# Tile addresses, load order and the head's instruction order in an SSD-scan and SiLU-MLP kernel on one core

## The chip, the cores and the metric

The kernel runs on one core of one Trainium2 chip. A core has a matrix engine (PE, whose weight loads are shown apart as PEld), a vector engine (DVE), an activation engine (ACT), a general engine (POOL) and a queue engine (SP) that issues transfers (DMA). The engines run side by side; each works through its own instructions in the order in which the program lists them, and waits where an operand isn't there yet. The metric is the device time in microseconds of one execution, the lower the better. It is given as the median of runs.

## The reference, cut to what matters

Two parts follow each other. The first is a state-space scan: for each of 4 batches and 8 heads, 768 positions with decay `a`, inputs `x` (32 wide), `B` and `C` (16 wide).

```python
log_a = np.log(np.clip(a, 1e-06, 1.0))
for c in range(nc):                       # chunks of the sequence
    la = log_a[:, :, sl]
    cum = np.cumsum(la, axis=-1)
    L = np.exp(cum[:, :, :, None] - cum[:, :, None, :]) * causal
    M = np.einsum('bhin,bhjn->bhij', Cc, Bc) * L
    y_intra = np.einsum('bhij,bhjd->bhid', M, xc)
    y_inter = np.einsum('bhin,bhnd->bhid', Cc, state) * decay_to_i
    y[:, :, sl] = y_intra + y_inter
    state = decay_full * state + np.sum(Bx, axis=2)
```

Its output, seen as 3072 rows of 256, goes through a two-layer network in float32:

```python
h = x @ w_in                              # (3072, 256) @ (256, 2048)
g = h * (1.0 / (1.0 + np.exp(-h)))
return g @ w_out                          # (3072, 2048) @ (2048, 256)
```

The weights arrive as float64, so that the kernel reads them as pairs of 32-bit words.

## The kernel before

**The scan.** The 3072 positions are cut into 12 units of 256 positions, three for each batch, and a unit into four chunks of 64. For each unit the kernel loads prefix inputs (`load_pa`, tile pz), decays with zeroed chunk starts (`load_ab`, tile ab), B and C (`load_n`, one layout, tiles bn and tbc; `load_t`, another layout, for the first unit of the first batch and from unit 3 on), and x (`load_x`, tile xt). The decays of units 2 and later come from two arrays in device memory, a_in and a_zero, which the kernel itself writes once, in `f_A2` (lines 246 to 253), after clipping `a` on DVE.

The letters in the schedule name a unit's steps. T is the transpose of B and C (`f_T` on DVE, L352, or `f_TP` on PE), with the two masked copies ce on ACT (L370). P is the prefix scan on DVE (L311), C multiplies C by it (L374, tile cw). The digits 1 and 2 are the two halves of the decay scan E on DVE (L324), B the product BT (L347). D is two groups of small matmuls on PE (`f_G` L402, `f_D0` L390). S updates the states on DVE (L420, L422), s masks them on ACT (L429), M multiplies into E on DVE (L408). Y is the output's matmuls on PE (L442, L451) and its copy to tile xf on ACT (L461). The letters h, l and d split xf into three parts, xh on ACT (L474) and xl, xd on DVE (L477, L481). These three parts of x, for two units together, are 4 KB per partition each and live in the pool `quad`, six buffers which they share with the raw weights.

**The weights.** They come in 16 slices of 256 columns or rows, eight for each layer: `load_w(n)` loads slice n into a `quad` buffer (512 KB), `w_size` prepares two words on ACT (L176, L179), `w_bits` combines them on DVE (L184, L186, L187) and adds on POOL (L192) to give a float32 slice. `w_bits(n)` also issues the load of slice n + 6, whose buffer it frees. `w_h`, `w_l` and `w_d` make three parts of the slice (wh on ACT, L199; wl and wd on DVE, L203 and L208), each a block of 2 KB per partition.

**The network.** The first two units, half an iteration, multiply float32 slices: `f_s1` (L491) for the first layer, `f_s2` (L504) for the second. A float32 matmul is two passes on PE, and each pass shows as one record. The ten units after them run as five iterations P of 16 steps each. A step works on 128 columns of the inner width and 512 positions, with float32r matmuls, which are one pass each: `s1_d` multiplies xd by wd (L518, 2 matmuls), ACT rescales (L520), `s1_h` adds xh by wh and xl by wl (L526, 4), ACT applies SiLU and splits (L534, L536), DVE or POOL make gl (L540) and DVE gd (L544). Three steps later `s2` multiplies gh by wh and gl by wl (L558, L559, 2 each), and `s2_d` multiplies gd by wd (L572, 2). In all of them the activations are the streamed operand and the weights the loaded one. `PLAN` and `FIRST` say which scan letters of the next two units are woven into which step, and `ASIDE` in which steps POOL makes gl.

The order is written out by hand. Below the line `w_size(5)` (680), the list `steps` gives pairs of a unit and a slice for `f_s1` and, as text, what follows each; a second list does the same around the `f_s2` calls (m0 to m5). In these texts "2:C12B" means the letters C, 1, 2 and B of unit 2, "L" a unit's loads, b, s, h, l and d with a number `w_bits`, `w_size`, `w_h`, `w_l` and `w_d`. All loads are issued by SP, in the order of the program, and a load whose buffer or source isn't ready holds up those behind it.

**Addresses.** The pools are laid out in the order in which they are created, so that a pool's place sets the addresses of those behind it. The parts of x and the raw weights (`quad`) begin at byte 32,576 of the partition, which is 832 past a multiple of 1024; the 76 blocks of 2 KB (pool `blk`, everything that `block()` makes: g's parts, the weights' parts, xf) begin at byte 72,576, 896 past a multiple of 1024. All sizes are multiples of 1024 from there, so every tile of a kind has the same offset.

Of the kernel before, what the change touches and what calls it, by code (L numbers as in the profile page):

```python
# [8 lines left out]
FP32 = mybir.dt.float32  # L9
# [24 lines left out]
def kernel(  # L34
# [26 lines left out]
    Q = 64  # L61
# [9 lines left out]
    loads = ctx.enter_context(tc.tile_pool(name="loads", bufs=1))  # L71
    quad = ctx.enter_context(tc.tile_pool(name="quad", bufs=6))
    sc = ctx.enter_context(tc.tile_pool(name="sc", bufs=1))
    sc2 = ctx.enter_context(tc.tile_pool(name="sc2", bufs=2))
    blk = ctx.enter_context(tc.tile_pool(name="blk", bufs=1))
    dram = ctx.enter_context(tc.tile_pool(name="dram", bufs=1, space=bass.MemoryType.DRAM))
    ps_s = ctx.enter_context(tc.tile_pool(name="ps_s", bufs=1, space=bass.MemoryType.PSUM))
# [3 lines left out]
    ctx.enter_context(tc.manual_schedule())  # L81

    NB = 76

# [18 lines left out]
    def load_pa(u, q):  # L103
        for c in range(4):
            q.dma_start(out=pz[:, c, 1:], in_=a_in[4 * u + c].rearrange("h (o t) -> h o t", o=1).to_broadcast([H, N, Q]))

# [16 lines left out]
    def load_t(u, i, q):  # L123
        b, t0 = at(u)
        if u == 0:
            tbc[u] = block("tbc0").rearrange("p (i e r n) -> p i e r n", i=2, e=2, r=8)
        elif u not in tbc:
            tbc[u] = loads.tile([128, 2, 2, 8, N], FP32, name="tbc")
        for g in range(4):
            q.dma_start(out=tbc[u][32 * g:32 * g + 32, i],  # L130
                        in_=(B, C)[i][b, 2 * g:2 * g + 2, t0:t0 + UT].rearrange("e (t r) n -> t e r n", r=8))

    def load_x(u, q):
        b, t0 = at(u)
        xt[u] = loads.tile([128, 2, H, D], FP32, name="xt", bufs=2)
        for k in range(2):
            q.dma_start(out=xt[u][:, k], in_=x[b, :, t0 + 128 * k:t0 + 128 * k + 128].rearrange("h p d -> p h d"))

    def load_unit(u):
        load_pa(u, nc.sync)  # L140
        if 0 < u < UPB:
            load_n(u, 1, nc.sync)
        else:
            load_t(u, 0, nc.sync)
            load_t(u, 1, nc.sync)
        load_n(u, 0, nc.sync)
        load_ab(u, nc.sync)
        load_x(u, nc.sync)
# [32 lines left out]
    def w_bits(n, parts=1):  # L181
        if n in raw:
# [7 lines left out]
            for i in range(parts):  # L190
                fs = slice(WF // parts * i, WF // parts * (i + 1))
                nc.gpsimd.tensor_tensor(out=two(w32[n])[:, :, fs].bitcast(U32), in0=u[:, :, fs], in1=v[:, :, fs],  # L192
                                        op=ALU.add)
        if n + RAW < NW:
            load_w(n + RAW, nc.sync)
# [15 lines left out]

    a_in = dram.tile([batch * S // Q, H, Q], FP32, name="a_in")
    a_zero = dram.tile([batch * S // Q, H, Q], FP32, name="a_zero")
# [32 lines left out]
    def f_A2():  # L246

        r = slice(0, NC0 * batch)
        nc.vector.tensor_scalar(out=acl[r], in0=acl[r], scalar1=1.0, scalar2=1e-6, op0=ALU.min, op1=ALU.max)
# [31 lines left out]
    tiny = const.tile([128, 1], FP32, name="tiny")  # L281
    nc.scalar.activation(tiny, idle[:, 0:1], AF.Silu)
    busy(5)
# [32 lines left out]
    def f_P(u):  # L316
        if u < 2:
            f_P0(u)
        f_P1(u)
# [15 lines left out]
    def f_Ek(u, k):  # L335
        scan_E(u, H * k, H, ab.pop((u, k)))
# [311 lines left out]
    f_Y(0)  # L648
    f_P(1)
    f_Ek(1, 0)  # L650
# [8 lines left out]
    f_s1(0, 1)  # L659
    f_Ek(1, 1)  # L660
    f_B(1)
    w_bits(2, 2)
# [19 lines left out]
    def stage(u, what):  # L682
        for c in what:
            if c == "L":
                load_unit(u)
            elif c == "T":
                if 0 < u < UPB:
# [31 lines left out]
            elif c == "d":  # L719
                f_xd(u)  # L720

    def todo(text):

        for step in text.split():
            if ":" in step:
                u, what = step.split(":")
                stage(int(u), what)
                continue
            n = int(step[1:].split(".")[0])
            {"b": w_bits, "s": w_size, "h": w_h, "l": w_l, "d": w_d, "m": f_s2, "o": f_out0}[step[0]](n)  # L730
# [24 lines left out]
    def step(s):  # L755
# [6 lines left out]
        if t >= 0:  # L762
            PENDING.append(t)
        if s == 0:
            s1_d(0)

        if s < last:
# [86 lines left out]
```

## Time and profile before

| | |
|---|---|
| median of 3 runs | 349.0 us (347.99 to 350.06) |
| the profiled execution's own time | 348.75 us |
| its span, first to last instruction | 346.5 us |
| granted PE clock, mean | 0.995 |
| PE busy | 324.6 us, 94% |
| DVE busy | 262.6 us, 76% |
| ACT busy | 211.9 us, 61% |
| POOL busy | 66.1 us, 19% |
| DMA, mean rate | 77 GB/s, 26.66 MB moved |

A busy time is the sum of an engine's instructions in the profiled execution. In a table of waits each row names the waiting engine, tile and line, then who released it, the total in microseconds, how often, and the longest. A piece of the chain has its start, its length and what ran; the pieces lie end to end, so that a piece of several matmuls divided by their number is the time from one start to the next. A matmul's own duration in the profile is longer than that, about 0.39 us, since matmuls overlap. L12 is line 12 of the kernel before.

### The profile page before, as it was taken

To read this page: it belongs to the slowest core of one execution; us is meant where nothing else is said; L and a number is where in the kernel's file an instruction comes from. 1 tells how busy PE (TensorE), PEld (TensorE's weight loads), DVE (VectorE), ACT (ScalarE), POOL (GpSimd) and SP (SyncE) were. 2 spreads that over 40 slices of the span, in tenths; PEclk is the share of its full clock that TensorE was granted. 3 is DMA by queue.
4 is the path that set the end of the run, shared out by engine and by line. 5 is a ranking of instruction groups with operands and counts; after the bars stand their busy time and mean duration, and the time that the engine had idled before them with its cause. 6 is when DMAs were issued, how large, how long until landed. Compare 5 with 4: busy or idle time off the path is not lost.

```text
span 346.5 us, 7826 instructions
## 1 busy us (share of the span) xinstructions
PE 324.6 (94%) x3145; PEld 254.3 (73%) x3146; DVE 262.6 (76%) x430; ACT 211.9 (61%) x403; POOL 66.1 (19%) x56
## 2 busy tenths in 40 slices
PE   8977999777998999999999999999999999999991
PEld 4566788666866778777778778778778788788881
DVE  7969975999559998898766896965996853674443
ACT  3656575432467877757775756666676756555651
POOL 3235523120113010242101231202250202000000
PEclk9999999999999999999999999999999999999998
DMA  6975894650171160045340163420153000020003
GB/s 121 209 248 173 168 335 98 145 115 0 48 144 25 38 117 1 18 108 83 67 97 0 34 120 67 88 63 1 48 112 57 2 2 0 0 48 14 0 0 63
DMA packets 99339, 26.66 MB, mean 77 GB/s; under 512 B 87558, under 2 KB 92422, under 8 KB 99302
## 3 DMA queue, kind: packets, MB, share of 16 engines
q1 hardware_dynamic: 95110, 25.76, 33.1%
q10 hardware_dynamic: 4192, 0.39, 0.9%
q8 instruction: 24, 0.39, 0.5%
q14 instruction: 13, 0.11, 0.1%
HBM read 22.80 MB, written 3.34 MB: 75 GB/s over the span
## 4 chain that ended last, share of the span: by engine, by line
PE 70%; DVE 10%; DMA 8%; SPq 8%; issue 2%; ACT 1%; DVEq 0%; ACTq 0%
PE hp L526 22%; PE b L572 11%; PE hp L518 10%; PE oa L559 10%; PE oa L558 10%; DMA raw<-in_moe_w_out_dram 3%; SPq L121 3%; PE oa L504 2%; DVE wl L203 2%; PE gy L451 2%; DMA ab<-a_zero 2%; PE gy L442 1%; DMA a_in<-acl 1%; DMA raw<-in_moe_w_in_dram 1%; PE gy L402 1%
## 5 line engine op out<-in xcount | busy, mean ns | idle before, releaser
L520 ACT ACTIVATE hp<-hp 128x512 f32<-128x512 f32 x80 | 46.6, 582 | 75.0 <-PE hp L518 74.7
L540 DVE TENSOR_TENSOR gl<-g,gh 128x512 fp32r<-128x512 f32 x56 | 38.6, 689 | 47.7 <-ACT gh L536 44.8
L540 POOL TENSOR_TENSOR gl<-g,gh 128x512 fp32r<-128x512 f32 x24 | 39.9, 1663 | 172.4 <-ACT gh L536 156.3
L526 PE MATMUL hp<-xh,wh 128*128 128x512 f32 x160 | 65.6, 410 | 2.6 <-ACT hp L520 2.6
L544 DVE SCALAR_TENSOR_TENSOR gd<-gh,g 128x512 fp32r<-128x512 f32 x80 | 61.9, 776 | 6.0 <-ACT gh L536 6.0
L526 PE MATMUL hp<-xl,wl 128*128 128x512 f32 x160 | 63.2, 395 | 0.0
L559 PE MATMUL oa<-gl,wl 128*128 128x512 f32 x160 | 63.1, 394 | 0.0
L558 PE MATMUL oa<-gh,wh 128*128 128x512 f32 x160 | 62.7, 392 | 0.0
L536 ACT ACTIVATE gh<-g 128x512 fp32r<-128x512 f32 x80 | 50.6, 632 | 2.8
L518 PE MATMUL hp<-xd,wd 128*128 128x512 f32 x160 | 50.4, 396 | 0.0
L534 ACT ACTIVATE g<-hp 128x512 f32<-128x512 f32 x80 | 47.5, 594 | 0.6 <-PE hp L526 0.6
L572 PE MATMUL b<-gd,wd 128*128 128x512 f32 x160 | 44.6, 391 | 0.0
L526 PEld LDWEIGHTS hp<-xh,wh 128*128 128x128 f32 x160 | 30.0, 188 | 13.0 <-ACT hp L520 6.0
L558 PEld LDWEIGHTS oa<-gh,wh 128*128 128x128 f32 x160 | 30.0, 188 | 7.5 <-ACT o L584 0.7
L518 PEld LDWEIGHTS hp<-xd,wd 128*128 128x128 f32 x160 | 30.0, 188 | 7.3
L559 PEld LDWEIGHTS oa<-gl,wl 128*128 128x128 f32 x160 | 30.0, 188 | 7.2
L572 PEld LDWEIGHTS b<-gd,wd 128*128 128x128 f32 x160 | 30.0, 188 | 6.8 <-DVE o L599 0.2
L526 PEld LDWEIGHTS hp<-xl,wl 128*128 128x128 f32 x160 | 30.1, 188 | 5.5
L491 PE MATMUL hp<-xf,w 128*128 128x256 f32 x128 | 30.1, 386 | 4.3 <-POOL w L192 3.0
L192 POOL TENSOR_TENSOR w<-wu,wv 128x512 uint32<-128x512 uint32 (+1 forms) x20 | 23.4, 1178 | 50.5 <-DVE wv L187 47.8
L491 PEld LDWEIGHTS hp<-xf,w 128*128 128x128 f32 x128 | 23.5, 190 | 9.7 <-POOL w L192 4.5
L324 DVE TENSOR_TENSOR_SCAN E<-ab,diag 128x512 f32<-128x512 f32 x24 | 28.7, 1228 | 0.7 <-DMA ab<-a_zero 0.7
(80 smaller groups left out, 367.0 us busy)
## 6 DMA issues: line engine op xcount, KB each, us to landing
ab<-a_zero SPq DMA_DIRECT2D x40, 128.0 KB
raw<-in_moe_w_in_dram SPq DMA_DIRECT2D x8, 512.0 KB
raw<-in_moe_w_out_dram SPq DMA_DIRECT2D x8, 512.0 KB
xt<-in_x_dram SPq DMA_DIRECT2D x24, 128.0 KB
out_dram<-ot SPq DMA_DIRECT2D x44, 64.0 KB
bn<-in_B_dram SPq DMA_DIRECT2D x22, 64.0 KB
tbc<-in_C_dram SPq DMA_DIRECT2D x40, 32.0 KB
pz<-a_in SPq DMA_DIRECT2D x40, 32.0 KB
```

Of the source, the lines that this page charges most:

```text
L324: nc.vector.tensor_tensor_scan(out=E[u].rearrange("p k h t -> p (k h t)")[:, Q * g0:Q * (g0 + n)], data0=t.rearrange("p g t -> p (g t)"), ...
L491: nc.tensor.matmul(out=hp[:, i], lhsT=two(w32[j])[:, kc, 128 * i:128 * i + 128], rhs=two(XF[u])[:, kc], start=(kc == 0), stop=(kc == KC - 1))
L518: nc.tensor.matmul(out=HP[s], lhsT=two(WD[f // 2])[:, kc, 128 * (f % 2):128 * (f % 2) + 128], rhs=XD[P][:, kc], start=(kc == 0), stop=Fals ...
L520: nc.scalar.activation(HP[s], HP[s], AF.Copy, scale=-HALF / UP)
L526: nc.tensor.matmul(out=HP[s], lhsT=two(w[f // 2])[:, kc, 128 * (f % 2):128 * (f % 2) + 128], rhs=x_[P][:, kc], start=False, stop=(kc == KC ...
L534: nc.scalar.activation(G[s], HP.pop(s), AF.Silu, scale=UP)
L536: nc.scalar.activation(GH[s], G[s], AF.Copy, scale=DOWN)
L540: engine.tensor_tensor(out=GL[s], in0=G[s], in1=GH[s].bitcast(FP32), op=ALU.subtract)
L544: nc.vector.scalar_tensor_tensor(out=GD[s], in0=GH[s].bitcast(FP32), scalar=1.0 + 1.0 / HALF, in1=G.pop(s), op0=ALU.mult, op1=ALU.subtract)
L558: nc.tensor.matmul(out=OA[P][m], lhsT=two(WH[n])[:, r, ms], rhs=gh, start=(f == 0), stop=False)
L559: nc.tensor.matmul(out=OA[P][m], lhsT=two(WL[n])[:, r, ms], rhs=gl, start=False, stop=(f == NF - 1))
L572: nc.tensor.matmul(out=B2[P][:, m], lhsT=two(WD[n])[:, r, 128 * m:128 * m + 128], rhs=gd, start=(fresh and s == tiles[0]), stop=True, skip ...
```

## The change

Four things are edited.

- The pool `quad` is created behind `blk`, and a tile of 160 bytes that nothing uses is added in pool `sc`; a tile of one element (`tiny`) is gone. The blocks then begin at byte 48,128 and the parts of x at byte 203,776, both multiples of 1024.
- `load_pa` becomes one transfer in place of four. For that a_in is laid out by head, with 65 values for each chunk, the first of them zero; `f_A2` writes the other 64, and a new transfer writes the zeros from a zeroed tile. `load_t` becomes two transfers in place of four.
- The loads of unit 2 and 3 are split and spread: C, B and x of unit 2 are issued ahead of slice 3's `w_bits` and of `f_A2`, its decays behind slice 4's; then C (with B in the layout of `load_t`) and x of unit 3; the decays and bn of unit 3 follow unit 2's scan ("3:A"). `w_bits` issues the next load only up to slice 4; slices 11 to 15 have their own letter r in the lists.
- In the head, unit 1's prefix scan stands behind its second decay scan, slice 3's `w_bits` before `f_A2`, unit 3's steps P, C, 1, 2 and B one place earlier and before slice 12's bits, its D before the second `f_s2`; the splits of unit 2 and 3 follow in another order; and the first `s1_d` (letter p) comes after m3 instead of after m5.

```diff
+    quad = ctx.enter_context(tc.tile_pool(name="quad", bufs=6))
+    sc.tile([128, 40], FP32, name="pad")
...
-        for c in range(4):
-            q.dma_start(out=pz[:, c, 1:], in_=a_in[4 * u + c].rearrange("h (o t) -> h o t", o=1).to_broadcast([H, N, Q]))
+        q.dma_start(out=pz.rearrange("p c t -> p (c t)"),
+                    in_=a_in[:, 4 * u:4 * u + 4].rearrange("h (o c) t -> h o (c t)", o=1).to_broadcast([H, N, 4 * Q + 4]))
...
-        for g in range(4):
-            q.dma_start(out=tbc[u][32 * g:32 * g + 32, i],
-                        in_=(B, C)[i][b, 2 * g:2 * g + 2, t0:t0 + UT].rearrange("e (t r) n -> t e r n", r=8))
+        src = (B, C)[i]
+        for e in range(2):
+            q.dma_start(out=tbc[u][:, i, e].rearrange("p r n -> p (r n)"),
+                        in_=bass.AP(tensor=src.tensor, offset=src.offset + ((b * H + e) * S + t0) * N,
+                                    ap=[[2 * S * N, 4], [8 * N, 32], [1, 8 * N]]))
...
+    def load_bcx(u, what="bcx"):
+        if "c" in what:
+            if 0 < u < UPB:
+                load_n(u, 1, nc.sync)
+            else:
+                load_t(u, 0, nc.sync)
+                load_t(u, 1, nc.sync)
+        if "b" in what:
+            load_n(u, 0, nc.sync)
+        if "x" in what:
+            load_x(u, nc.sync)
...
-        if n + RAW < NW:
+        if n < 5:
             load_w(n + RAW, nc.sync)
...
-    a_in = dram.tile([batch * S // Q, H, Q], FP32, name="a_in")
+    a_in = dram.tile([H, batch * S // Q, Q + 1], FP32, name="a_in")
...
-        nc.sync.dma_start(out=a_in, in_=acl[r])
+        nc.sync.dma_start(out=a_in[:, :, 1:].rearrange("h c t -> c h t"), in_=acl[r])
...
+    nc.sync.dma_start(out=a_in[:, :, 0:1].rearrange("h c t -> c h t"),
+                      in_=misc[:NC0 * batch, 0:H].rearrange("p (h t) -> p h t", t=1))
...
-    f_P(1)
     f_Ek(1, 0)
...
     f_Ek(1, 1)
+    f_P(1)
...
+    load_bcx(2)
+    w_bits(3, 2)
     f_A2()
-    load_unit(2)
     w_size(4, "u")
-    w_bits(3, 2)
...
     w_bits(4)
+    load_pa(2, nc.sync)
+    load_ab(2, nc.sync)
+    load_bcx(3, "cx")
     w_size(5)
...
+            elif c == "A":
+                load_pa(u, nc.sync)
+                load_bcx(u, "b")
+                load_ab(u, nc.sync)
...
-    steps = ((1, 0, ""), (0, 3, "b5 s6"), (1, 1, "b6 s7"), (1, 2, "b7 s8"), (1, 3, "b8"), (0, 4, "2:T"),
-             (1, 4, "2:P"), (0, 5, "2:C12B s9 3:L"), (1, 5, "2:D b9 s10"), (0, 6, "2:SsM"), (1, 6, "b10 s11"),
-             (0, 7, "2:Y b11 s12 3:T"), (1, 7, "b12 s13 3:P h0"))
+    steps = ((1, 0, ""), (0, 3, "b5 r11 s6"), (1, 1, "b6 s7"), (1, 2, "b7 s8"), (1, 3, "b8"), (0, 4, "2:T"),
+             (1, 4, "2:P"), (0, 5, "2:C12B s9 3:A r12 r13"), (1, 5, "2:D b9 r14 r15 s10"), (0, 6, "2:SsM"), (1, 6, "b10 s11"),
+             (0, 7, "2:Y b11 s12 3:T"), (1, 7, "3:PC12B b12 s13 h0"))
...
-    for text in ("m0 3:C12B 2:h h1 l0 d0 2:l b13 s14", "m1 3:D 2:d 4:L h2 l1 d1 b14 s15", "m2 3:SsM h3 l2 d2 b15",
-                 "m3 3:Y h4 l3 d3", "m4 3:h h5 l4 d4 h8 3:l", "m5 3:d l5 d5 4:T l8 d8"):
+    for text in ("m0 3:D 4:L 3:SsM 2:h h1 2:l 2:d l0 d0 b13 s14", "m1 h2 l1 d1 b14 s15", "m2 3:Y 3:h l2 d2 3:l 3:d b15 h3",
+                 "m3 l3 d3 h4 p0", "m4 h8 l4 d4 h5 l8 d8", "m5 4:T l5 d5"):
...
-        if s == 0:
-            s1_d(0)
```

More of the change, by code (lines that the diff above doesn't have):

```diff
@@ L71 @@
     loads = ctx.enter_context(tc.tile_pool(name="loads", bufs=1))
-    quad = ctx.enter_context(tc.tile_pool(name="quad", bufs=6))
     sc = ctx.enter_context(tc.tile_pool(name="sc", bufs=1))
@@ L137, in load_x @@
             q.dma_start(out=xt[u][:, k], in_=x[b, :, t0 + 128 * k:t0 + 128 * k + 128].rearrange("h p d -> p h d"))
+    def load_bcx(u, what="bcx"):
[9 more added lines that the diff above has]
+            load_x(u, nc.sync)
     def load_unit(u):
         load_pa(u, nc.sync)
[L141 to L146, printed above, removed]
+        load_bcx(u, "bc")
         load_ab(u, nc.sync)
@@ L280 @@
                                 fill=1.0, base=-64 * c, channel_multiplier=1)
-    tiny = const.tile([128, 1], FP32, name="tiny")
-    nc.scalar.activation(tiny, idle[:, 0:1], AF.Silu)
+    nc.scalar.activation(misc[:, 2 * UT - 1:], idle[:, 0:1], AF.Silu)
     busy(5)
@@ L720, in stage, with load_r @@
                 f_xd(u)
+    def load_r(n):
+        load_w(n, nc.sync)
     def todo(text):
@@ L729, in todo @@
             n = int(step[1:].split(".")[0])
-            {"b": w_bits, "s": w_size, "h": w_h, "l": w_l, "d": w_d, "m": f_s2, "o": f_out0}[step[0]](n)
-    steps = ((1, 0, ""), (0, 3, "b5 s6"), (1, 1, "b6 s7"), (1, 2, "b7 s8"), (1, 3, "b8"), (0, 4, "2:T"),
-             (1, 4, "2:P"), (0, 5, "2:C12B s9 3:L"), (1, 5, "2:D b9 s10"), (0, 6, "2:SsM"), (1, 6, "b10 s11"),
-             (0, 7, "2:Y b11 s12 3:T"), (1, 7, "b12 s13 3:P h0"))
+            {"b": w_bits, "s": w_size, "h": w_h, "l": w_l, "d": w_d, "m": f_s2, "p": s1_d, "r": load_r}[step[0]](n)
+    steps = ((1, 0, ""), (0, 3, "b5 r11 s6"), (1, 1, "b6 s7"), (1, 2, "b7 s8"), (1, 3, "b8"), (0, 4, "2:T"),
+             (1, 4, "2:P"), (0, 5, "2:C12B s9 3:A r12 r13"), (1, 5, "2:D b9 r14 r15 s10"), (0, 6, "2:SsM"), (1, 6, "b10 s11"),
+             (0, 7, "2:Y b11 s12 3:T"), (1, 7, "3:PC12B b12 s13 h0"))
     for u, j, text in steps:
```

## The prediction

> **What bounds the kernel now.** I read four views, in this order: the busy shares, the busy time by stretch (columns: time, PE, weight loads, DVE, ACT, POOL, clock, DMA share, GB/s), the waits of PE and DVE in the head, and the chain that ended last.
>
> ```profile
> PE 324.6 (94%) x3145; PEld 254.3 (73%) x3146; DVE 262.6 (76%) x430; ACT 211.9 (61%) x403; POOL 66.1 (19%) x56
> ...
> 97.28:107.44 10.16, 8.76 (x95) 6.03 (x95) 8.37 (x15) 7.55 (x15) 2.87 (x2) 1.00 0.59 117
> 107.44:126.90 19.46, 19.46 (x224) 15.25 (x224) 19.25 (x30) 16.15 (x33) 3.00 (x2) 1.00 0.22 49
> 126.90:147.30 20.40, 20.40 (x179) 16.48 (x179) 17.80 (x29) 14.37 (x28) 2.44 (x2) 1.00 0.15 28
> 147.30:157.55 10.25, 10.25 (x104) 7.65 (x102) 10.11 (x17) 6.39 (x13) 4.73 (x3) 1.00 0.56 114
> 157.55:176.95 19.40, 19.40 (x225) 15.17 (x224) 15.68 (x26) 13.85 (x28) 3.04 (x2) 1.00 0.40 79
> ```
>
> From 107.44 us to the last matmul PE is never idle, at full granted clock: there only cheaper matmuls shorten the run. But DVE is as full as PE in two stretches (19.25 of 19.46, 10.11 of 10.25); there a faster PE will meet DVE. Before that, PE waits (who for whom: total us, times, longest):
>
> ```profile
> PE gy L442 <- DVE E L408: 4.5, 4, 2.3
> PE hp L491 <- POOL w L192: 3.0, 3, 1.8
> PE hp L526 <- ACT hp L520: 2.6, 2, 1.9
> PE gy L390 <- DVE BT L347: 2.1, 1, 2.1
> ...
> DVE acl L249 <- DMA acl<-in_a_dram: 2.6, 1, 2.6
> DVE bh L352 <- DMA tbc<-in_B_dram: 2.5, 1, 2.5
> DVE ct L352 <- DMA tbc<-in_C_dram: 1.2, 1, 1.2
> DVE E L324 <- DMA ab<-a_zero: 0.7, 1, 0.7
> ```
>
> PE waits for DVE's products, and DVE stands 7.0 us for late inputs. What a matmul costs is in the chain's pieces (start, length, what), which lie end to end:
>
> ```profile
> 91.76 3.45 PE oa L504 x16
> ...
> 288.50 0.93 PE hp L526 x4
> 289.44 0.47 PE hp L518 x2
> ...
> 335.37 0.23 PE oa L558
> ...
> 337.63 0.92 PE b L572 x4
> ```
>
> L504 is fp32: each matmul is two passes of 256 columns, two cycles a column, thus 512 cycles a pass; it takes 3.45/16 = 215.6 ns. The fp32r matmuls (L518, L526, L558, L559, L572) stream 512 columns once, so also 512 cycles. They take longer: those that stream the parts of x (L526, L518) 0.93/4 and 0.47/2, about 233 ns; those that stream g's parts, with no x part between them, (338.55 - 335.37)/14 = 227.1 ns. A whole step of 12 takes 2.78 us (L526 starts at 285.73 and 288.50), 231.7 ns each.
>
> **The change, tile addresses.** The Trainium skill ("TensorE: Matmul & The Clock Gate", Wait — 56ns, not 53.3ns?) gives 215.7 ns for 512 columns back to back at 2.4 GHz. The fp32 row agrees; the fp32r rows do not. At 2.4 GHz, 233.3 ns is 560 cycles and 226.7 ns is 544: 48 and 32 cycles too many. The parts of x begin 832 bytes past a multiple of 1024, so 192 bytes, or 48 columns, lie before the next multiple. The blocks of 2 KB that hold g's parts begin 896 past: 128 bytes, 32 columns. Both agree if columns before the first such boundary stream at half speed; fp32, at two cycles a column anyway, would not notice, and it doesn't. This is my reading of two offsets; no row has a third. After the change both kinds begin at a multiple of 1024, so I take 215.7 ns, which is page and fp32 row at once. By the rows as they stand it would be 231.7 and the edit worth nothing.
>
> Of the 960 fp32r matmuls (six groups of 160), 910 start after 107.44 us: 910 x 16.0 ns = 14.6 us. Not all arrives:
> - 107.44 to 126.90: DVE works without a gap to its product L408 (done 126.60), and PE starts L442 at 126.91. PE would gain 72 x 16 = 1.2 us here; DVE allows 0.3. Lost: 0.9.
> - DVE is also gapless from 144.29 to 157.39, where L408 ends 0.16 us before PE needs it. 51 matmuls lie there: gain 0.8, allowed 0.1. Lost 0.7, and again at 207.57 and 257.65, where the margins are 0.4 and 0.15: about 2.0 in all.
> - Elsewhere DVE has idle to give (15.68 of 19.40 us busy, and a margin of 1.9 us at 176.95).
> That leaves 14.6 - 0.9 - 2.0 = 11.7 us. The 29 matmuls of 97.28 to 107.44 give nothing: DVE is gapless from 98.97 to 107.29 and PE already waits 1.35 us. The 19 of 85.24 to 97.28 give 0.3.
>
> **The change, the head.** Step by step, on PE's clock:
> - DVE's prefix scan for unit 1 (L307, L311: 0.3 + 1.1 us) moves behind unit 1's second scan. Weight slice 1 comes 1.3 us sooner, so PE's 1.03 us wait at 17.94 goes; but DVE does the same work before its product at 23.50, and PE waits there instead. Nothing.
> - Slice 3's bits move ahead of f_A2. In the kernel before, DVE waits 2.57 us for acl, to 26.07, and does the bits from 27.00. Now they fall into that wait: done about 25, POOL's halves about 26.7, when PE is busy to 27.59. PE's 1.85 us wait (27.59 to 29.45) goes. f_A2 now waits for slice 3 and has slices 4 to 8 behind it, as before.
> - But PE's product of unit 0 and slice 5 at 41.53 waits for unit 2's cw, behind DVE's bits of slices 4 to 8. These start about 1.4 us sooner, so PE gets 1.4, not 1.85.
> - SP: six issues (C, B, x of unit 2; 0.6 each, 3.6 us) now stand before a_in's write, and one of 384 packets of 4 bytes is new. a_in is issued about 29.1, not 26.5. Landing took 4.87 us, so unit 2's prefix load (one issue for four) starts about 34, its ab's four at 34.6 to 37.2, and ab lands about 39: 39.56 before. Hidden behind DVE's slices.
> - a_in is now written in 256-byte pieces. A rule speaks against it: "DMA: Bandwidth & Descriptors", Specifications, asks for 512 bytes, below which there is a read-modify-write. The trace's 256-byte packets at 34 us took 17.6 ns each, so 384 on 16 engines cost 0.4 us, against 4.87 us of landing. By the rule, taken as a doubled landing, ab would land at 44, unit 2's BT would come at 47 and PE would wait 4 us. I take the row and keep 4 us for the range.
> - Unit 3's C, B and x are issued at 37 to 41 and a's parts after unit 2's scans, before raw slices 12 to 15. In the kernel before, six slices of 512 KB go first (the chain has 9.93 us of raw from 43.47), and tbc's two halves and ab land at 55, 57 and 62.7. Now ab lands about 48.5. Slice 11 and later are delayed by 1 to 5 us but their bits come later still.
> - So DVE's 2.54 + 1.21 + 0.70 us of waiting go, and unit 3's scans stand before slice 12's bits: slice 11's bits end at 52.6 - 1.4 = 51.2, then transposes, prefix, cw, scans and BT take 5.1: done about 56.3. PE's unit 3 products move ahead of the second L504 slice, so it needs BT at about 57.5. Both waits (2.06 at 64.51, 2.29 at 74.36) go: 4.35 us.
> - The first L518 pair moves two slices earlier, so ACT's L520 lies behind 7 us of L504 and the 1.94 us wait at 85.24 goes. But the pair needs unit 3's xd. DVE has from 57.8, by durations of before: products 2.3, two xl/xd pairs 2.4, three wl/wd pairs 3.6, two slices' bits 2.8, two POOL blocks of 1.1: to 71.1. PE is there at 69.6. A new wait of 1.5 (0 to 2.5); gain 0.4. Behind it PE's queue holds the last two slices.
> - 20 load issues per unit become 13. In the loop SP mostly waits for stores (84 us): nothing. The pad and the Silu's new target: nothing.
>
> Head: 1.4 + 4.35 + 0.4 = 6.2 us; between 2 (rule for a_in) and 8.5 (no new waits).
>
> **Sum.** The profiled execution took 348.75 us for a span of 346.5; the median is 349.0. 348.75 - 11.7 - 0.3 - 6.2 = 330.55; on the median's basis 330.8, say **331**. Own range: loop 9.5 to 16 (all of DVE's holds released and the 2.5 ns floor gone), head 2 to 8.5: 326 to 337.
>
> **Rivals.**
> - *Only x's parts were misplaced.* A fixed 32 cycles belong to every fp32r matmul, and 64 bytes off a multiple of 128 cost 16 more. The two offsets fit this as well; the clean 544 cycles speak for it, but no fp32 pass has such a surcharge. 442 x 6.7 ns = 2.9 us: 349 - 2.9 - 6.2 = 340.
> - *Addresses do nothing:* the surcharge comes from weights or the target bank. Against it: L558 and L526 both load weights from blocks, yet differ. 349 - 6.2 = 343.
> - *Slower: an aligned start pays a full period* instead of none, 128 columns if it repeats every 512 bytes. Two offsets don't exclude it. 266.7 ns, +35 x 910 = +32 us: 375. It decides from 239 ns on, where it eats the head's gain (7 x 910 = 6.4); a 256-byte period (240 ns) would give 350.
> - *The head gives nothing*, a_in late: 331 + 6 = 337, the own range's upper end.
>
> **How the numbers follow.** My reading 0.78, only x's parts 0.09, nothing 0.06, full period 0.07 (half slower, half near zero). 326 to 337 holds about nine tenths of the first; reaching to 340 takes in half of the second: 326 to 340. A measurement here can tell 0.5%, 1.7 us. Faster 0.93, same 0.03, slower 0.04.
>
> **What would show it.** Right: the chain's L526 x4 at 0.86 us, L572 x8 at 1.73, a step at 2.59; PE waits on L408 near 120, 150, 198 and 247 us of 0.7 to 1; none on BT L347; DVE no longer waiting for tbc. Wrong: steps still at 2.7 or more; a DVE wait for ab of unit 2; a long L518 wait.

## The result, and the profile after

The changed kernel takes 344.06 us (median of 4 runs, 343.19 to 345.07); the kernel before, run beside it, 349.24 (4 runs, 347.99 to 350.06). The ratio is 0.9856 (95% interval 0.9812 to 0.99): 1.4% faster, 5 us. The forecast was 331, with a range from 326 to 340. The sign was right; the size was not, by 13 us.

The profiled execution took 345.07 us for a span of 343.4, 3.1 us less than before. It was the slowest of the four; the spans of the others were 341.4 to 341.7. The profiled execution of before was one of its better ones: of 27 executions of that kernel beside the first experiments, the seven with a mean granted clock of 0.994 or more have a median of 348.6 us and the nine under 0.9885 one of 351.0, which fits medians that gain more (5.2 us) than the two traces (3.1).

The page's busy shares of the changed kernel:

```profile
PE 323.2 (94%) x3146; PEld 256.6 (75%) x3146; DVE 261.8 (76%) x430; ACT 211.6 (62%) x403; POOL 63.6 (19%) x56
```

PE was to lose some 12 us of work. It lost 1.4, with some 3 us of slower passes, shown below, added to it. Its pieces of the chain, with start and length, say what became of the matmuls (L529, L537, L569, L570, L583 are L518, L526, L558, L559, L572 of before; the head's and loop's lines lie 10 or 11 higher in the changed kernel; the loads' L121 is L122, L137 is L140):

```profile
283.22 0.91 PE hp L537 x4
284.12 0.45 PE hp L529 x2
...
285.94 0.91 PE hp L537 x4
286.84 0.45 PE hp L529 x2
...
288.66 0.91 PE hp L537 x4
...
334.14 0.92 PE b L583 x4
```

The step, from one L537 to the next, is 2.72 us, 226.7 ns for each of 12 matmuls, where the forecast had 2.59. The matmuls that stream x's parts came down from 233.3 to 226.7 ns (0.91/4, 0.45/2). Those that stream g's parts, with no x part between them, took 0.92 for four before and take 0.92 still.

The waits that end on PE's and DVE's critical work (who for whom: total us, times, longest):

```profile
PE hp L502 <- DVE cw L385: 3.3, 1, 3.3
DVE pfx L322 <- DMA pz<-a_in: 3.1, 1, 3.1
PE gy L453 <- DVE E L419: 2.1, 2, 1.4
PE hp L529 <- DVE xd L492: 1.5, 1, 1.5
PE hp L537 <- ACT hp L531: 0.7, 1, 0.7
```

The waits on BT, on POOL's slices and most of ACT's rescaling are gone, as forecast. The first two rows are new. PE's timeline shows what they cost (start, us, line, operands; in brackets the idle time before and who ended it):

```profile
37.75 1.99 PE L502 MATMUL hp<-xf,w 128*128 128x256 f32 x8 [0.25 <-ACT gT L505]
43.08 6.64 PE L502 MATMUL hp<-xf,w 128*128 128x256 f32 x16 [3.34 <-DVE cw L385]
49.65 0.69 PE L413 MATMUL gy<-ce,bh 32*64 32x128 f32 x32
...
77.40 0.73 PE L529 MATMUL hp<-xd,wd 128*128 128x512 f32 x2 [1.47 <-DVE xd L492]
...
84.69 0.58 PE L537 MATMUL hp<-xh,wh 128*128 128x512 f32 x1
...
106.90 0.69 PE L453 MATMUL gy<-cw,sm 32*64 32x64 f32 x32 [1.43 <-DVE E L419]
```

The product of unit 0 and slice 5 starts at 43.08, where it was to start at 40.1 (before: 41.53). And it takes 6.64 us, where the same 16 passes took 3.69 before. The stretches of time show the reason in the third value from the end, the granted clock (0.66 in the second row; columns as in the prediction):

```profile
30.00:40.00 10.00, 9.49 (x45) 7.82 (x43) 8.33 (x11) 7.61 (x15) 5.64 (x5) 1.00 0.81 182
40.00:50.00 10.00, 6.92 (x40) 5.42 (x48) 5.37 (x8) 2.33 (x5) 0.38 (x1) 0.66 0.63 169
50.00:60.00 10.00, 10.00 (x183) 8.39 (x165) 7.68 (x16) 7.21 (x16) 3.46 (x3) 1.00 0.83 244
```

At 49.65 PE is 4.5 us behind the kernel before (45.16). It catches up, since no later wait is left in the head but that for xd. The first L537 starts at 84.69 against 85.24: the head gave 0.55 us of its 6.2.

So the 3.1 us of the two spans are: 0.55 in the head; nothing from there to the matmuls L453 of unit 4 (22.21 us against 22.20); 2.95 in the loop, from those (106.90, before 107.44) to the last matmul (335.57, before 339.06); and 0.4 lost in the last stores.

Why the prefix came late is in SP's timeline of the changed kernel (start, us, what it issues, how many):

```profile
25.14 2.90 SPq L122 DMA_DIRECT2D tbc<-in_C_dram  x2
28.09 4.27 SPq L122 DMA_DIRECT2D bn<-in_B_dram  x2
32.46 1.16 SPq L140 DMA_DIRECT2D xt<-in_x_dram  x2
...
34.34 0.41 SPq L262 DMA_DIRECT2D a_in<-acl  x1
...
38.76 0.62 SPq L105 DMA_DIRECT2D pz<-a_in  x1
```

The six issues ahead of a_in's write took 8.33 us, not 3.6. DVE had acl ready at 26.1; a_in was issued at 34.34, its landing took 4.40, that of pz 2.90 more: 41.68. In the kernel before there are two sets of rows for the same issues, one while the weights' first slices are being moved and one when the queues are light:

```profile
8.16 2.31 SPq L121 DMA_DIRECT2D bn<-in_B_dram  x2
10.51 4.15 SPq L121 DMA_DIRECT2D tbc<-in_C_dram  x2
...
35.10 1.21 SPq L121 DMA_DIRECT2D bn<-in_B_dram  x2
```

The forecast took the last one. Three slices of 512 KB had just been issued at 23.6 to 24.7 us, so the first two were the ones to take: 2.31 + 4.15 + 1.21 for x is 7.7.

### The profile page after: what moved, and what is told of

Same layout as the page of the kernel before. It is cut to its first block, busy times and chain, and to the rows that moved or that the text cites. A ratio compares the mean times of both kernels' runs of the same rounds, so it can differ in the third digit from the quotient of the medians.

```text
span 343.4 us, 7744 instructions
## 1 busy us (share of the span) xinstructions
PE 323.2 (94%) x3146; PEld 256.6 (75%) x3146; DVE 261.8 (76%) x430; ACT 211.6 (62%) x403; POOL 63.6 (19%) x56
## 3 DMA queue, kind: packets, MB, share of 16 engines
HBM read 22.82 MB, written 3.34 MB: 76 GB/s over the span
## 4 chain that ended last, share of the span: by engine, by line
PE 80%; DVE 8%; SPq 4%; DMA 3%; ACT 1%; issue 1%; DVEq 0%; ACTq 0%
PE hp L537 21%; PE b L583 11%; PE hp L529 10%; PE oa L569 10%; PE oa L570 10%; PE hp L502 6%; PE oa L515 5%; PE gy L462 2%; PE gy L453 2%; SPq L122 2%; PE gy L413 2%; DVE wd L218 1%; SPq L180 1%; DMA a_in<-acl 1%; DMA raw<-in_moe_w_in_dram 1%
## 5 line engine op out<-in xcount | busy, mean ns | idle before, releaser
L551 POOL TENSOR_TENSOR gl<-g,gh 128x512 fp32r<-128x512 f32 x24 | 38.2, 1594 | 169.6 <-ACT gh L547 146.8
L537 PE MATMUL hp<-xh,wh 128*128 128x512 f32 x160 | 65.2, 407 | 0.7 <-ACT hp L531 0.7
L569 PE MATMUL oa<-gh,wh 128*128 128x512 f32 x160 | 62.5, 391 | 0.1
L537 PE MATMUL hp<-xl,wl 128*128 128x512 f32 x160 | 62.5, 391 | 0.0
L570 PE MATMUL oa<-gl,wl 128*128 128x512 f32 x160 | 62.3, 389 | 0.0
L529 PE MATMUL hp<-xd,wd 128*128 128x512 f32 x160 | 49.5, 390 | 1.5 <-DVE xd L492 1.5
L583 PE MATMUL b<-gd,wd 128*128 128x512 f32 x160 | 44.3, 390 | 0.0
L502 PE MATMUL hp<-xf,w 128*128 128x256 f32 x128 | 32.6, 412 | 5.5 <-DVE cw L385 3.3
L537 PEld LDWEIGHTS hp<-xh,wh 128*128 128x128 f32 x160 | 30.0, 188 | 10.3 <-ACT hp L531 3.7
L529 PEld LDWEIGHTS hp<-xd,wd 128*128 128x128 f32 x160 | 30.0, 188 | 8.3 <-DVE xd L492 1.9
L569 PEld LDWEIGHTS oa<-gh,wh 128*128 128x128 f32 x160 | 30.0, 188 | 6.9 <-ACT o L595 0.7
L583 PEld LDWEIGHTS b<-gd,wd 128*128 128x128 f32 x160 | 30.0, 188 | 6.5 <-DVE o L610 0.3
L570 PEld LDWEIGHTS oa<-gl,wl 128*128 128x128 f32 x160 | 30.0, 188 | 6.2
L502 PEld LDWEIGHTS hp<-xf,w 128*128 128x128 f32 x128 | 25.8, 207 | 11.1 <-issue 3.7
L537 PEld LDWEIGHTS hp<-xl,wl 128*128 128x128 f32 x160 | 30.1, 188 | 5.2
L202 POOL TENSOR_TENSOR w<-wu,wv 128x512 uint32<-128x512 uint32 (+1 forms) x20 | 22.6, 1136 | 53.4 <-DVE wv L197 53.4
L515 PE MATMUL oa<-gT,w 128*128 128x256 f32 x128 | 28.8, 381 | 0.0
```

Source lines behind the costliest of these rows:

```text
L502: nc.tensor.matmul(out=hp[:, i], lhsT=two(w32[j])[:, kc, 128 * i:128 * i + 128], rhs=two(XF[u])[:, kc], start=(kc == 0), stop=(kc == KC - 1))
L515: nc.tensor.matmul(out=OA[0][m][:, UT * u:UT * u + UT], lhsT=two(w32[8 + j])[:, i, 128 * m:128 * m + 128], rhs=two(GT[u, j])[:, i], start= ...
L529: nc.tensor.matmul(out=HP[s], lhsT=two(WD[f // 2])[:, kc, 128 * (f % 2):128 * (f % 2) + 128], rhs=XD[P][:, kc], start=(kc == 0), stop=Fals ...
L537: nc.tensor.matmul(out=HP[s], lhsT=two(w[f // 2])[:, kc, 128 * (f % 2):128 * (f % 2) + 128], rhs=x_[P][:, kc], start=False, stop=(kc == KC ...
L551: engine.tensor_tensor(out=GL[s], in0=G[s], in1=GH[s].bitcast(FP32), op=ALU.subtract)
L569: nc.tensor.matmul(out=OA[P][m], lhsT=two(WH[n])[:, r, ms], rhs=gh, start=(f == 0), stop=False)
```

## The experiments: the addresses

**The addresses alone.** The kernel before with `quad` behind `blk` and a pad of 128 bytes, so that all these tiles begin at multiples of 1024.

```diff
-    quad = ctx.enter_context(tc.tile_pool(name="quad", bufs=6))
     blk = ctx.enter_context(tc.tile_pool(name="blk", bufs=1))
+    quad = ctx.enter_context(tc.tile_pool(name="quad", bufs=6))
...
+    sc.tile([128, 32], FP32, name="pad")
```

> The kernel before with the new tile addresses and nothing else. If only the 64 bytes off a multiple of 128 cost anything (16 cycles a matmul, for L518 and L526 alone), these matmuls go from 233 to 226.7 ns, the others stay at 226.7, a step takes 2.72 us in place of 2.78, and the run is 2.5 to 3 us faster than before (346.3). If the 1024-byte boundary of the prediction mattered in any part, some matmuls would come at 215.7 ns and the gain would exceed 8 us. The head up to the first L526 (85.2 us) should not move.

Measured: 345.8 us against 350.21, ratio 0.9883 (0.9848 to 0.9918), thus 4.1 us (2.9 to 5.3). The step is 2.72 us, the first of x's and wh's matmuls comes at 85.24 as before, the span is 343.7. All of the loop's gain is here. Its span is 2.8 us under that of before, less than the medians' 4.1, as with the whole change. Pieces of its chain (its L527 is L526 of before), and behind them a wait and the passes that follow it in PE's timeline:

```profile
283.76 0.91 PE hp L527 x4
...
286.48 0.91 PE hp L527 x4
```

```profile
64.49 0.68 PE L391 MATMUL gy<-xt,BT 64*32 64x64 f32 x32 [1.85 <-DVE BT L348]
65.10 8.58 PE L505 MATMUL oa<-gT,w 128*128 128x256 f32 x32
```

In before these passes take 7.17 us. So here the clock fell (0.83 from 60 to 70 us), which it did not in the trace of before.

**All but the addresses.** The changed kernel with the pools at their former offsets.

```diff
     loads = ctx.enter_context(tc.tile_pool(name="loads", bufs=1))
+    quad = ctx.enter_context(tc.tile_pool(name="quad", bufs=6))
...
-    sc.tile([128, 40], FP32, name="pad")
+    const.tile([128, 1], FP32, name="gap")
```

> The changed kernel with its tiles at the old offsets (832 and 896 past 1024). The head alone: if the two parts simply add, 344.1 + 2.8 = 346.9 us, 2.3 us under the kernel before, the step back at 2.78 us. The wait for the prefix load (L322 in the changed kernel) and the stretch of low PE clock after it should be there as in the changed kernel. If the stretch comes from the addresses, it is gone and the run is below 344.

Measured: 348.97 us against 350.21, ratio 0.9962 (0.9942 to 0.9982): 1.3 us, where 2.3 was expected. The step is 2.78 us again. In the profiled execution PE waited 5.45 us for cw where the changed kernel waited 3.34, its next 16 passes took 6.37, and the first L537 came at 86.67:

```profile
45.34 6.37 PE L502 MATMUL hp<-xf,w 128*128 128x256 f32 x16 [5.45 <-DVE cw L385]
```

The two halves of the change add up: 4.1 + 1.3 is 5.4, against 5.0 to 5.2 of the whole.

**Other offsets.** The changed kernel with the 2 KB blocks 32 bytes past a multiple of 1024 and x's parts 96 past.

```diff
+    gap = ctx.enter_context(tc.tile_pool(name="gap", bufs=1))
+    gap.tile([128, 16], FP32, name="gap")
     quad = ctx.enter_context(tc.tile_pool(name="quad", bufs=6))
...
-    sc.tile([128, 40], FP32, name="pad")
+    sc.tile([128, 48], FP32, name="pad")
```

> The changed kernel with the 2 KB tiles (weights and g's parts) at 32 bytes past a multiple of 1024 and x's parts at 96 past. Theory A, a rule in multiples of 128 bytes that costs by distance: 64 off cost 16 cycles, so 32 off costs 8 (230 ns) and 96 off costs 8 to 24 (230 to 237 ns). Theory B, any odd multiple of 32 or 64 bytes costs the same 16 cycles: both at 233.3 ns. Theory C, only an odd multiple of 64 costs: both at 226.7 ns, as with multiples of 1024. A step of 12 at 2.72 us (C), 2.76 (A), 2.80 (B).

The chain of this kernel in one execution (L539 and L585 are the L537 and L583 of the others):

```profile
280.89 1.82 PE b L585 x8
...
285.49 0.93 PE hp L539 x4
...
288.26 0.93 PE hp L539 x4
...
291.03 0.93 PE hp L539 x4
```

A step of 2.77 us, 231 ns each: nearest to a cost that grows with the distance (2.76), and neither nothing (2.72) nor the full 16 cycles (2.80). But the first row is the other half of the matter: g's parts with no x part between them take 1.82/8 = 227.5 ns at 32 past, about what they take at 0 (227). So the mixed step costs nearly what it did before, and the run doesn't say whether x's 96 or g's 32 is to blame. Nor does any run have x's parts at an odd multiple of 128: every mixed step without a surcharge had all its tiles at multiples of 1024, and that 128 is the period stays the rival's reading.

**Multiples of 2048, and another type.** The changed kernel with the tiles at multiples of 2048 bytes and 24 bf16 matmuls of 512 columns at the end, which are additional work.

```diff
-    sc.tile([128, 40], FP32, name="pad")
-    NB = 76
+    sc.tile([128, 296], FP32, name="pad")
+    NB = 75
...
     for s in range(NF * (NP - 1) + LAG):
         step(s)
+    busy(24)
```

> The changed kernel with the tiles at multiples of 2048 bytes, and with 24 more bf16 matmuls of 512 columns at its end, which are additional work (about 5.5 us). If the 32 cycles over 512 are still an address effect, of a larger period than 1024, fp32r matmuls fall to 215.7 ns and the loop shortens by 10 us. If they belong to fp32r matmuls whatever the address, a step stays at 2.72 us (226.7 ns each), and the bf16 ones show whether other types have them too: 215.7 ns each if only fp32r pays, 226.7 if every single pass of 512 columns pays.

The end of its chain in one execution, the last fp32r matmuls and then the bf16 ones:

```profile
333.39 0.91 PE b L583 x4
...
335.27 5.13 PE zero L274 x23
```

The fp32r matmuls stay at 0.91/4, 227 ns. The bf16 ones, whose records are 0.38 us long each, start (5.13 - 0.38)/22 = 215.9 ns apart. Same engine, same clock, same 512 columns: the 11 ns between them go with fp32r and not with an address, as far as multiples of 1024 and 2048 can show it. An fp32r column is also twice as many bytes as a bf16 one, and the run doesn't separate the two. This is the fixed part in the rival that the prediction gave 0.09.

## The experiments: the head

**a_in's write first.** The changed kernel with unit 2's C, B and x behind `f_A2`.

```diff
-    load_bcx(2)
     w_bits(3, 2)
     f_A2()
+    load_bcx(2)
```

> The changed kernel, only that C, B and x of unit 2 are issued behind f_A2 and not ahead of it. Theory: the six issues held SP from 25.1 to 33.6 us, so that a_in was issued at 34.3, pz landed at 41.7, PE waited 3.3 us and then ran 6.6 us in place of 3.5 at a low clock. Then a_in is issued near 27, PE's wait at 43 falls below 0.5 us (if C and B of unit 2 are still in time), the clock stays at 1.00, the first L526 comes near 79 instead of 84.7 and the run takes 338 to 340. Rival: a_in's 256-byte pieces or DVE's order set the head; then the wait shrinks by less than 1 us and the run stays at 343 to 345.

Measured: 344.55 us, ratio to before 0.9836 (0.9804 to 0.9868): no better than the changed kernel, a miss. a_in was issued at 27.61, 6.7 us sooner, but the prefix load was not. SP's timeline and the waits of this kernel:

```profile
28.50 3.41 SPq L122 DMA_DIRECT2D tbc<-in_C_dram  x2
31.95 3.18 SPq L122 DMA_DIRECT2D bn<-in_B_dram  x2
...
37.13 0.63 SPq L105 DMA_DIRECT2D pz<-a_in  x1
```

```profile
PE hp L502 <- DVE cw L385: 4.6, 1, 4.6
DVE pfx L322 <- DMA pz<-a_in: 4.3, 1, 4.3
```

The stall only changed places: it stood in front of a_in's write and now stands in front of pz, which landed at 42.9.

**The wait filled.** The changed kernel with 20 bf16 matmuls of 512 columns, additional work whose result nobody reads, in PE's wait before the product of unit 0 and slice 5.

```diff
     for u, j, text in steps:
+        if (u, j) == (0, 5):
+            fill(20)
         f_s1(u, j)
```

> The changed kernel with 20 bf16 matmuls of 512 columns, whose result nothing uses, where PE waits for unit 2's cw (43 us). Theory: the 3.3 us wait stays, but the clock doesn't fall, so the 16 L502 passes behind it take 3.5 us and not 6.6: first L526 near 81.5, run near 341. Rival: the 6.6 us come from the transfers or weights and not from the clock; then the run stays at 344. If the fill is longer than the wait it costs its excess: 20 x 0.22 = 4.3 us against 3.3 + 0.0.

Its stretch from 40 to 50 us:

```profile
40.00:50.00 10.00, 10.00 (x98) 6.85 (x97) 6.81 (x12) 3.83 (x7) 1.28 (x1) 1.00 0.55 138
```

The clock stays at 1.00 and the 16 passes take 3.45 us between starts instead of 6.64, although they begin 0.8 us later. So the fall of the clock follows PE's idling; the late prefix alone would not have cost it. The time, 344.07 us (ratio 0.9828, 0.9799 to 0.9857), hardly moved, where some 341 was expected: of 2.2 us won at 47.43, 1.4 went again, most of it in a wait of 1.15 us for unit 3's ce (ACT stood 3.7 us waiting for a raw slice), and the first L537 came at 83.87.

**The prefix before the bulk.** The changed kernel with all of unit 2's loads behind `f_A2`, the prefix first, and raw slices 9 and 10 behind them.

```diff
-        if n < 5:
+        if n < 3:
             load_w(n + RAW, nc.sync)
...
-    load_bcx(2)
     w_bits(3, 2)
     f_A2()
+    load_pa(2, nc.sync)
+    load_bcx(2, "bc")
+    load_ab(2, nc.sync)
+    load_bcx(2, "x")
+    load_w(9, nc.sync)
+    load_w(10, nc.sync)
...
-    load_pa(2, nc.sync)
-    load_ab(2, nc.sync)
     load_bcx(3, "cx")
```

> The changed kernel, with unit 2's loads behind f_A2 (a_in's write, the prefix load, C, B, ab, x) and raw slices 9 and 10 behind those. Theory 1, the head's gain was lost because the prefix load stood behind stalled issues and bulk on SP: DVE's prefix scan starts by 40 us instead of 41.7, PE's product of unit 0 and slice 5 at about 40 instead of 43.1, no fall of the granted clock in 40 to 50, the first L537 at 78 to 80 instead of 84.7, and 338 to 340 us. Theory 2, DVE (gapless from 62 to 87) and the raw slices bound the head's end anyway: the scan is early, the clock stays full, and the first L537 still comes at 83 to 84, PE waiting for xd of unit 3 or for wh; 342.5 to 344 us.

Measured: 346.22 us against 349.79, ratio 0.989 (0.9862 to 0.9918). Its profiled execution took 344.05 and was the fastest of six; the others took 345.6 to 347.3 at a lower mean clock (0.980 to 0.987 against 0.992), so the trace shows the best case, and the median lies above the times of both theories. Theory 1 fell. Theory 2's picture came in that trace: the scan early (38.27, no wait), the clock full, the first L537 at 83.07. Of the two causes it names, ACT's timeline shows the slices, which had made way:

```profile
47.05 0.66 ACT L186 ACTIVATE wu<-raw 128x512 f32<-128x512 f32 x1 [3.57 <-DMA raw<-in_moe_w_out_dram]
...
59.12 0.66 ACT L186 ACTIVATE wu<-raw 128x512 f32<-128x512 f32 x1 [4.07 <-DMA raw<-in_moe_w_out_dram]
```

**And the first pair later.** The same with the first L529 pair one L515 slice later ("m4 p0" for "m3 ... p0").

> The kernel of the run before (prefix before bulk) with the first L529 pair one L515 slice later, behind m4 instead of m3. Its wait for unit 3's xd (1.5 us in the changed kernel, 1 to 4 in the run before) goes, and ACT's L531 still lies behind one L515 slice. Theory 1: 1 to 1.5 us faster than the run before, about 337 to 339 us. Theory 2 (DVE's last wl and wh set the first L537): the wait only moves to L537, no more than 0.3 us.

Measured: 345.17 us, ratio 0.9863 (0.984 to 0.9886), where 337 to 339 was expected. PE's timeline of this kernel has no wait for xd, but another:

```profile
61.34 1.16 PE L413 MATMUL gy<-ce,bh 32*64 32x128 f32 x32 [4.15 <-ACT ce L381]
```

ACT's ce of unit 3 stood behind its step for slice 12, which waited 4.82 us for that slice. PE's clock fell behind the wait, its next 32 passes took 9.52 us in place of 7.17, and the first L537 came at 84.52.

**The bulk taken out.** These runs all say that something is late, each time something else. If that is the volume of the transfers, it goes when the volume goes. Slices 9 to 15 are not loaded here; their bits are made from slice 8's raw tile, and all other instructions stay. Once on the order with the prefix before the bulk:

```diff
+        if n > 8:
+            raw[n] = raw[8]
+            return
         t = raw[n] = quad.tile([128, 2, WF, 2], U32, name="raw", tag="quad")
```

> The kernel with the prefix before the bulk, but raw slices 9 to 15 are not loaded: their bits are made from slice 8's raw tile, so 3.5 MB of transfers are left out and every other instruction stays. Theory 2 (volume): no DVE or ACT wait for a transfer over 0.5 us between 38 and 62 us, full clock, first L537 at 78 to 79.5 (5 to 6 us before the changed kernel's 84.7), a span of 336.5 to 338. If DVE's work bounds the head's end whatever arrives: 81.5 to 83.

```profile
71.66 0.73 PE L532 MATMUL hp<-xd,wd 128*128 128x512 f32 x2 [1.48 <-DVE xd L495]
...
78.94 0.58 PE L540 MATMUL hp<-xh,wh 128*128 128x512 f32 x1
```

PE's timeline has one wait over 0.3 us left between 38 and 79, that for xd, of the forecast's length; the first of the loop's matmuls (L540 here) starts 6.3 us before the kernel before's. The span is 337.6, as expected. Without these loads neither DVE nor ACT waits over 0.5 us for a transfer in that stretch. And once on the changed kernel's own order:

> The changed kernel's own order, but raw slices 9 to 15 are not loaded (slice 8's tile stands in for them), 3.5 MB left out. If slices 9 and 10 ahead of the prefix load make it late, pz lands by 39 and the first L537 comes at 79 to 80.5. If the stall is in the issues of unit 2's C, B and x in small packets behind slices 6 to 8 (8.3 us on SP), which stay, a_in is still issued at about 34 us, pz lands after 40.5, PE still waits 2 us or more for cw, its clock falls, and the first L537 comes at 82 to 84.

```profile
41.36 5.38 PE L505 MATMUL hp<-xf,w 128*128 128x256 f32 x16 [2.08 <-DVE cw L388]
```

Here SP's issues of C and B still took 2.70 and 4.52 us, a_in was issued at 33.80, pz was waited for until 39.95, the clock fell (0.83 from 40 to 50 us), and the first of the loop's matmuls came at 81.71, between what the two accounts expected. Both have a share, by one execution of each of the two kernels: of the 5.75 us between the changed kernel (84.69) and the head without bulk (78.94), 3.0 go with the slices 9 to 15 and then 2.8 with the order of unit 2's loads, which stand behind slices 6 to 8.

**By need.** All bytes moved again, in the order in which they are wanted: slice 9 into the time in which a_in lands, then unit 2, slices 10 and 11, C and B of unit 3, slice 12, x, prefix, B and ab of unit 3, slices 13 to 15.

```diff
     f_A2()
+    load_w(9, nc.sync)
+    load_pa(2, nc.sync)
+    load_bcx(2, "bc")
+    load_ab(2, nc.sync)
+    load_bcx(2, "x")
...
-    load_pa(2, nc.sync)
-    load_ab(2, nc.sync)
-    load_bcx(3, "cx")
+    load_w(10, nc.sync)
...
-    steps = ((1, 0, ""), (0, 3, "b5 r11 s6"), (1, 1, "b6 s7"), ...
+    steps = ((1, 0, ""), (0, 3, "b5 r11 3:c s6"), (1, 1, "b6 r12 3:x s7"), ...
-             ... (0, 5, "2:C12B s9 3:A r12 r13"), ...
+             ... (0, 5, "2:C12B s9 3:A r13"), ...
```

> The changed kernel with the head's transfers in the order in which they are needed: a_in's write, raw slice 9 (into the time in which a_in lands), the prefix load, C, B, ab, x of unit 2, raw 10, 11, C, B of unit 3, raw 12, x of unit 3, its prefix, B and ab, raw 13 to 15. Theory 1, the order was the fault: pz in time, ACT's waits for raw 9, 11 and 12 (3.6, 1.3 and 4.1 us in the run with the prefix before the bulk) mostly gone, first L537 at 79 to 81, 339 to 341 us. Theory 2, the head's transfers are more than the queues carry in 25 to 60 us, so that any order makes something late: one of pz, raw 9 to 12, unit 3's C, B or ab is waited for by 2 us or more, first L537 at 82.5 to 84.5, 342.5 to 344.5 us.

Measured: 343.79 us against 350.14, ratio 0.9826 (0.9792 to 0.9861). In the profile DVE waited 1.8 us for ab, PE 1.47 us for unit 3's BT and 2.13 for xd (behind slice 13, for which ACT waited 4.24), the clock fell, the first L537 came at 83.27: the second theory's picture. With the first pair later:

> The run before (order by need) with the first L529 pair one L515 slice later. Theory 1: the wait for xd goes and the first L537 comes 1 to 1.5 us sooner, 338 to 340 us. Theory 2 (PE is held before the pair, as where the prefix stood before the bulk): no more than 0.5 us, 342 to 344.5 us.

Measured: 342.7 us, ratio 0.976 (0.9713 to 0.9807), in two groups: 339.63 and 339.96 us with a mean granted clock of 0.997 and 0.996, the other four 342.5 to 343.9 with 0.990 to 0.992. PE's timeline of one of the four:

```profile
62.27 0.46 PE L401 MATMUL gy<-xt,BT 64*32 64x64 f32 x32 [3.28 <-DVE BT L358]
62.66 8.86 PE L515 MATMUL oa<-gT,w 128*128 128x256 f32 x32
```

A wait of 3.28 us for BT, and 1.7 us more for the fallen clock (8.86 against 7.17). That again is the second theory's picture, and two of the six are near the first one's time.

**The scans before slice 12.** The last kernel names what is late in the one before and moves only that: unit 3's prefix, B and ab go ahead of slice 12 and of x; ACT takes slice 12 behind unit 3's ce and slice 13 behind unit 2's xh.

```diff
-(1, 1, "b6 r12 3:x s7") ... "2:C12B s9 3:A r13" ... "2:Y b11 s12 3:T" ... "3:PC12B b12 s13 h0"
+(1, 1, "b6 s7") ... "2:C12B s9 3:A r12 3:x r13" ... "2:Y b11 3:T" ... "3:PC12B s12 b12 h0"
-"m0 3:D 4:L 3:SsM 2:h h1 2:l 2:d l0 d0 b13 s14"
+"m0 3:D 4:L 3:SsM 2:h h1 s13 2:l 2:d l0 d0 b13 s14"
```

> The order by need with the later first pair, changed in three places: unit 3's prefix, B and ab go ahead of raw slice 12 and x of unit 3; ACT's Abs and Copy of slice 12 stand behind unit 3's cw, and those of slice 13 behind unit 2's xh. Theory 1, an order exists in which the same bytes stay hidden: PE's wait for unit 3's BT (3.3 us in the run before it) is under 1 us, the clock stays full to 84 us, the first L537 comes at 79.5 to 81 (78.9 with the bulk taken out), 339 to 341 us in every execution. Theory 2, with all bytes moved something is late in any order: another wait of 2 us or more on PE between 36 and 80 us, the first L537 at 82.5 to 84, 342 to 344 us.

Measured: 338.25 us (337.99 to 338.76, 6 runs) against 350.28, ratio 0.9659 (0.9621 to 0.9697). It beats both kernels, and the 339 to 341 that was expected. PE's timeline:

```profile
57.35 0.69 PE L413 MATMUL gy<-ce,bh 32*64 32x128 f32 x32
...
58.81 0.35 PE L401 MATMUL gy<-xt,BT 64*32 64x64 f32 x16 [0.31 <-DMA xt<-in_x_dram]
59.09 7.17 PE L515 MATMUL oa<-gT,w 128*128 128x256 f32 x32
...
74.31 0.81 PE L529 MATMUL hp<-xd,wd 128*128 128x512 f32 x2
...
78.23 0.58 PE L537 MATMUL hp<-xh,wh 128*128 128x512 f32 x1
```

No wait over 1.5 us is left between 30 and 84, the clock stays at 1.00, and the loop begins 7.0 us before the kernel before's. The same bytes fit: it was the order, in the head's second half as well as in its first. What was moved on SP and on ACT was moved together; which part of it did how much is not shown.

## Why the prediction was wrong, point by point

**The addresses.** The step that failed is "Both agree if columns before the first such boundary stream at half speed", and with it "I take 215.7 ns, which is page and fp32 row at once". Two offsets with two surcharges allowed a line through nothing and a line through a constant. The text said so, and then took the first, because "no fp32 pass has such a surcharge". But an fp32 pass is another kind of matmul, as a bf16 one is, and neither can tell what fp32r costs at best. The Trainium skill's 215.7 ns ("TensorE: Matmul & The Clock Gate", Wait — 56ns, not 53.3ns?) is matched by bf16 here (215.9) and by the fp32 passes (215.6), and by no fp32r matmul (226.7). The term 910 x 16.0 = 14.6 us, less the holds, was to bring 11.7 + 0.3; the loop gave 2.95 by the trace. The rival's 442 x 6.7 ns is 2.96. Its picture is not exact either: a step without scan work became some 60 ns shorter, where six x matmuls at 6.7 are 40, so some of g's matmuls beside x's had paid too. As 2.95 us over 910 matmuls are 39 ns a step, the steps with scan work must have gained less. What divides the two stays open.

**DVE's holds.** Waits of 0.7 to 1 us on L419 near 120, 150, 198 and 247 us were to show; none over 0.1 us came, since matmuls that are 5 ns cheaper in place of 16 hardly catch up with DVE. At 126 us PE now starts 0.15 us behind DVE's product (0.31 before). Whether 16 ns would have been held up was not put to a test.

**The head, what was right.** Slice 3's bits fell into the wait for acl, and POOL's wait of 1.85 us went. Both waits, 4.35 us together, for unit 3's BT and E went, but in part by luck: BT came at 62.23 and not about 56.3, and was in time because PE, which was to need it about 57.5, came at 63.42. In the order by need, with PE early, PE stood 1.47 and 3.28 us for it again. ACT's 1.94 us before the first L526 went. The new wait for xd was 1.47 us, forecast 1.5, with both engines some 6 us later than forecast. a_in's 256-byte pieces landed in 4.40 us, before 4.87: the row was right, the rule of 512 bytes did not show. And 6.2 us was the head's size when its inputs came in time: 6.3 without the bulk, 7.0 in the last kernel, which saves the 1.5 for xd too.

**The head, what failed.** The step is "six issues (C, B, x of unit 2; 0.6 each, 3.6 us) now stand before a_in's write". They took 8.33. "a_in is issued about 29.1" became 34.34, and the prefix load, which was to start "about 34" and so to land ahead of DVE, free at 38.61, started at 38.76: from there on it was the input that PE stood for. The text followed ab alone to its reader, and called it hidden. Missing from the sum, put at nothing without a reason, was what a wait does to the clock: 3.34 us of idling cost PE some 3 us more in the 16 passes behind it. Last, "Slice 11 and later are delayed by 1 to 5 us but their bits come later still" held in the changed kernel only because PE was late itself (ACT waited 0.25 us); where the prefix came in time, ACT waited up to 5.5 us for a slice.

**The range.** 340 was the lower rival's place with the head's gain in full. The two misses came together, which no case in the list held. The own range's ends are not worked out alike either: 349 - 9.5 - 2 is 337.5, but 349 - 16 - 8.5 is 324.5 and not 326. The head's lower bound of 2 us, from one rule on one transfer, left out the stall that the trace of before showed at 8.16.

## What to carry to other kernels

A surcharge that two readings explain equally well is settled by one matmul of another type at the same place, before it is multiplied by 900. An issue is priced by the row that stands under the same load on the queues, and an input is followed to its first reader on every engine, since an order that makes one transfer early makes another late. A wait of some 2 us on PE can cost most of its length again in clock, so waits are removed in the order in which they come, until none is long enough for that.

## What the runs showed of the hardware

- fp32r matmuls of 512 columns start 226.7 ns apart with all tiles at multiples of 1024 bytes, and 227 with them at multiples of 2048; bf16 ones start 215.9 ns apart.
- With x's parts 64 bytes off a multiple of 128 (832 past a multiple of 1024) the matmuls that stream them take 233.3 ns, at multiples of 1024 226.7. g's parts with no x part between them take 227 to 228 ns at 0, 32 and 896 past. A mixed step of 12 takes 2.72 us at multiples of 1024, 2.78 with the offsets of before, and 2.77 with 32 and 96.
- PE's clock fell behind waits of 5.45, 4.58, 4.15, 3.34, 3.28, 2.13, 2.08 us, and in the run with the addresses alone behind one of 1.85 (32 passes in 8.58 us, not 7.17). It did not fall behind 2.06 and 2.29 in the traced execution of before, or behind 1.82 to 1.97 elsewhere. So the wait's length alone doesn't decide it, and the loss doesn't grow with it: 16 passes after 4.58 us took 5.12 us, after 3.34 us 6.64, where the kernel before took 3.69 for them at full clock. That other executions of before, with a lower mean clock, lose it behind its two waits is likely, but none of them has a trace here. After the wait of 3.34 us a pass took 6.64/16 = 415 ns on average, about twice 215.6, which agrees with the half rate that the Trainium skill names ("TensorE: Matmul & The Clock Gate", Part 1: The HAM clock gate); its idle window of about 3.4 us does not, as waits of little more than half of that were enough.
- 20 bf16 matmuls in that wait kept the granted clock at 1.00, and the 16 passes behind it took 3.45 us.
- Two issues of C or B by SP took 1.1 to 1.2 us with the queues light and mostly 2.0 to 4.8 us behind slices of 512 KB (one pair directly behind three slices took 1.23).
